# First hop of a graph propagation kernel: two-block groups at both ends, and one-hots that keep their place in program order

## The chip, the cores and the metric

The kernel runs on one core of one Trainium2 chip. A core has a matrix engine (PE, with its weight loads shown apart as PEld), a vector engine (DVE), an activation engine (ACT), a general engine (POOL) and a queue engine (SP) that starts transfers. The metric is the device time of one execution in microseconds, as the median of several runs. A profile of one execution gives the times of single instructions.

## The reference

Seven hops of a normalised sum over the edges of a graph, then a small attention over the eight vectors that each node has, and a readout. N is 10,000 nodes, E 160,000 edges, D 128. The hops are all that matters here.

```
h = x
toks = [x]
for _ in range(K):                                   # K = 7
    msg = h[src] * deg_inv_sqrt[src, None] * deg_inv_sqrt[dst, None]
    h = _segment_sum(msg, dst, N)
    toks.append(h)
tok = jnp.stack(toks, axis=1)                        # (N, K+1, D)
t = _layernorm(tok, axis=-1)
...
return jnp.einsum('nk,nkd->nd', alpha, o)
```

## The kernel before

The edges are sorted first, by source and by destination block, into cells (pass A and a decode, 0 to 394 us). A hop then works on blocks of 128 destination nodes: 78 blocks (NW) and a last remainder block. For a block, matmuls with selection matrices gather the source rows out of the table in on-chip memory (L667, into `p`), copies bring them to 16 bits (`eb`, L670, on ACT or DVE), and matmuls with a second set of selection matrices add them into the sum of the block (`acc`, L645). Edges for which a cell has no room are fetched row by row from DRAM (`og`, L591, on POOL) by an index `oidx`, and added by L631 and L658 (with the matrix `Sov`). `finish` (L617) adds the two halves of the sum on DVE, and L696 to L698 write the table's new rows and the row maximum `mx`.

The first hop builds these selection matrices (`w`, both sets in one tile) while it runs, and stores them to DRAM (`gsd`), from where hops 2 to 7 load them. It works in groups of blocks, called quads in the code: 20 groups, of blocks 72–75, 76–77, then 0–3, 4–7 up to 68–71. Iteration q of the loop runs four generators, a step of each in turn: `place` for group q+1, `left_out` for group q, `matrices` for group q, and the hop itself (`hop1`) for group q−1.

`place` takes the blocks of a group in pairs. For a pair, on each engine:

- DVE: the one-hot `oh` of the cell of each edge (128 x 3800 numbers; L396, made in `onehot`, L204), in a pool with two buffers
- PE: the counts of each cell, 25 matmuls (L400); ACT copies them to H (L401); PE makes their running sums (L406); ACT copies them to U (L408)
- DVE: `ux`, the one-hot times U (L217); PE sums over the cells (L222, L223); DVE reduces to the rank `rk` of each edge in its cell (L226)
- DVE: the one-hot of the rank and two products with it (`R`, L204 and L210), then the edges without room (`vo`, L423; L425)
- PE: the matrix of cells times ranks, 50 matmuls (L420) from `oh` and `R`; ACT copies it to `tbs` (L421)

At the end of a group the table goes to DRAM (`srow`, L430), and PE spreads it (L434, L436); DVE writes `oidx` (L439). `left_out` starts with the flags `fl` (L448), once a group, and gives the index and the matrix for the edges without room (L451 to L481, with `ohp` at L204 and matmuls at L473). `matrices` reads the rows back (`rb`, L555) and writes `w`: the gather half by L582 on DVE or two activations on ACT (L578), the scatter half by L571 and L583 on DVE. `w` has five buffers. `place_end` (up to L544) does the like for the edges of the remainder block at the end, with twelve one-hots `ohp` and matmuls L537.

Each engine runs its instructions in one fixed order. A scheduler of the language sets it, from its own estimate of when each instruction's inputs are ready; an instruction may be moved ahead of others that the program states first. `keep_in_program_order(x)` ties an instruction behind the one that the program stated just before it on the same engine.

Of the kernel before, what the change touches and what calls it, by code (L numbers as in the profile page):

```python
# [15 lines left out]
ALU = mybir.AluOpType  # L16
# [6 lines left out]
NG = 18  # L23
# [9 lines left out]
NS = 4 * NJ  # L33
# [3 lines left out]
NW = NT - 1  # L37
NE = 3
# [5 lines left out]
class Hops:  # L44
# [152 lines left out]
        V.tensor_scalar(self.ctok[0], self.disT, self.sinv, None, op0=ALU.mult)  # L197


    def onehot(self, pool, name, key, n, oh=None):  # L200
        m = key.shape[1]
        if oh is None:
            oh = pool.tile([128, m, n, 2], F16, name=name)
        self.nc.vector.tensor_tensor(oh, key[:, :, None, :].to_broadcast([128, m, n, 2]),  # L204
                                     self.io2[:, None, :n, :].to_broadcast([128, m, n, 2]), op=ALU.is_equal)
        return oh

    def times(self, out, oh, f):
# [160 lines left out]

    def pb_open(self, c):  # L370
        tc, V = self.tc, self.nc.vector
        self.bwp = c.enter_context(tc.tile_pool(name="bw", bufs=2))
        self.bw1 = c.enter_context(tc.tile_pool(name="bw1", bufs=1))
        self.pU = c.enter_context(tc.tile_pool(name="pU", bufs=1, space=PSUM))
        tm = c.enter_context(tc.tile_pool(name="psm", bufs=1, space=PSUM)).tile([128, 2, 128], F32, name="tm")
        self.tb, self.msc = tm[:NS, 0, :].rearrange("p (g r) -> p g r", g=2), tm[:, 1, :]

        cp = self.bp
        es = cp.tile([NS, 4, NJ], I32, name="es")
        self.nc.gpsimd.iota(es, pattern=[[1, 4], [4, NJ]], base=0, channel_multiplier=-1)  # L380
        self.io4 = cp.tile([128, 32, 2], F16, name="io4")
        V.tensor_copy(self.io4, self.iof[:, :32, None].to_broadcast([128, 32, 2]))
        self.pidn = cp.tile([128, 1], F32, name="pidn")
        V.tensor_scalar(self.pidn, self.pid1, -STEEP, 1.0, op0=ALU.mult, op1=ALU.add)
        self.esel = cp.tile([NS, 4, NJ], F16, name="esel")
        V.tensor_scalar(self.esel, es, 0.0, None, op0=ALU.is_equal)

    def place(self, ts, got):

        tc, nc, V, A, T, G = self.tc, self.nc, self.nc.vector, self.nc.scalar, self.nc.tensor, self.nc.gpsimd  # L390
        wp, w1, n = self.bwp, self.bw1, len(ts)
        tbs = wp.tile([NS, 4, 64], F16, name="tbs")
        ov = wp.tile([128, 4, 8], F32, name="ov")
        for p0 in range(0, n, 2):
            cols = lambda z: z[:, :, ts[0] + p0:ts[0] + p0 + 2]
            oh = self.onehot(wp, "oh", cols(self.kB), NS)  # L396
            ur = self.pU.tile([128, 512], F32, name="ur")
            H = wp.tile([128, NS, 2], F16, name="H")
            for c in range(NCH):
                T.matmul(ur[:, :2 * NS], self.id16, oh[:, c], start=c == 0, stop=c == NCH - 1)  # L400
            A.copy(H, ur[:, :2 * NS].rearrange("p (k i) -> p k i", i=2))  # L401
            yield
            U = ur[:, 512 - 2 * NS:].rearrange("p (k i) -> p k i", i=2)
            h = NS // 4
            for w in range(4):
                T.matmul(U[:, w * h:(w + 1) * h], self.triw[:, w, :], H[:, w * h:(w + 1) * h], start=True, stop=True)  # L406
            U2 = wp.tile([128, NS, 2], F16, name="U2")
            A.copy(U2, U)  # L408
            yield
            yield from self.rank(wp, w1, ur, oh, U2, cols(self.wB))  # L410
            rk = self.rk
            R = w1.tile([128, NCH, 2 * CAP, 2], F16, name="R")
            ro = self.onehot(w1, "R", rk, CAP, R[:, :, :CAP])
            self.times(R[:, :, CAP:], ro, cols(self.dl))
            self.times(ro, ro, cols(self.sl))
            yield
            tb = self.tb
            for g in range(2):
                for c in range(NCH):
                    T.matmul(tb[:, g, :], oh[:, c, :, g], R[:, c, :, g], start=c == 0, stop=c == NCH - 1)  # L420
            A.copy(tbs[:, p0:p0 + 2, :], tb)  # L421
            vo = wp.tile([128, NCH, 2], F32, name="vo")
            V.scalar_tensor_tensor(vo, rk, float(CAP), cols(self.TT), op0=ALU.is_ge, op1=ALU.mult)  # L423
            for g in range(2):
                V.max(ov[:, p0 + g, :], vo[:, :, g])  # L425
            yield
        n, a, b = len(ts), ts[0], ts[-1] + 1
        msc = self.msc

        nc.sync.dma_start(self.srow[a:b, :].rearrange("t (s r) -> s t r", r=CAP), tbs[:4 * NG, :n, 0:CAP])  # L430
        dsl = wp.tile([128, 4, NJ], I32, name="dsl")
        for g in range(n):
            for q in range(4):
                T.matmul(msc[32 * q:32 * q + 32, 32 + g * NJ:32 + (g + 1) * NJ], tbs[:, g, CAP:2 * CAP], self.esel[:, q, :],  # L434
                         start=True, stop=True, tile_position=(0, 32 * q))
                T.matmul(msc[32 * q:32 * q + 32, 16 + g * NI:16 + (g + 1) * NI], tbs[:, g, 0:CAP], self.esel[:, q, NG:],  # L436
                         start=True, stop=True, tile_position=(0, 32 * q))
        A.activation(dsl[:, :n, :], msc[:, 32:32 + n * NJ].rearrange("p (g j) -> p g j", j=NJ), AF.Copy, bias=-1.0)
        V.tensor_scalar(self.oidx[:, a:b, :NI], msc[:, 16:16 + n * NI].rearrange("p (g i) -> p g i", i=NI), -1.0, 0.0, op0=ALU.add, op1=ALU.max)  # L439
        got += [dsl, ov]  # L440
# [266 lines left out]
    def run(self, ctx, beside, nhop=K):  # L707
        tc, nc, V, A, T, G = self.tc, self.nc, self.nc.vector, self.nc.scalar, self.nc.tensor, self.nc.gpsimd
        with ExitStack() as c:
# [2 lines left out]
            G.memset(self.TT[:, :, NK:], 0.0)  # L712
            self.pass_a()
            self.decode()
            self.gsp = c.enter_context(tc.tile_pool(name="gs1", bufs=5))
            self.pg = c.enter_context(tc.tile_pool(name="pg1", bufs=4, space=PSUM))
            self.pacc = c.enter_context(tc.tile_pool(name="pc1", bufs=2, space=PSUM))
            self.ogp = c.enter_context(tc.tile_pool(name="og1", bufs=2))
            self.fp = c.enter_context(tc.tile_pool(name="fp1", bufs=1))
            self.pb_open(c)  # L720
            self.more_ebufs(c.enter_context(tc.tile_pool(name="eb1", bufs=1)), 5, True)
            pend = []
# [4 lines left out]
                self.next_rows(t, s, self.tab[1], self.c1[1], self.mx[0], 1, nc.sync)  # L727
                self.token_out(1, t, s, self.ctok[0])

            quads = [list(range(a, min(NW, a + 4))) for a in (4 * NG, 4 * NG + 4, *range(0, 4 * NG, 4))]  # L730
            dsl, W, nq = [[] for _ in quads], [[] for _ in quads], len(quads)

            def hop1(q):
                for t, w in zip(quads[q], W[q]):
                    og = [self.fetch(t, j, (self.tabd[0], self.tabh[0])) for j in range(NI + 1)]
                    yield from self.block(t, w, self.tab[0], lambda og=og: og, pend, 4, (4, 5), True,
                                          lambda jj: q < nq - 1 or jj in (0, 2, 4, 5, 7), fin1, t == quads[0][0])
                    if t == quads[-1][1]:
                        pend.append(lambda: self.end_block(True, fin1))

            for _ in self.place(quads[0], dsl[0]):
# [1 line left out]
            for q in range(nq + 1):  # L743
                pl = self.place(quads[q + 1], dsl[q + 1]) if q + 1 < nq else self.place_end() if q + 1 == nq else iter(())
                lf = self.left_out(quads[q], dsl[q][1]) if q < nq else iter(())
                if q + 1 == nq:
                    pl, lf = chain(lf, pl), iter(())
                if q == nq:
                    for k in range(NE):
                        self.fetch_end(k, self.tabd[0])  # L750
                if q == 0:
                    mt = self.matrices(quads[0], dsl[0][0], W[0])
                    next(mt)
                hp = hop1(q - 1) if q else iter(())
                for i in range(16):
                    if i % 2 == 0:
                        next(hp, None)
                    if i % 3 != 1:
                        next(pl, None)
                    if i % 2 == 1:  # L760
                        next(lf, None)
                    if i in (1, 3, 7, 9, 11, 15):
                        next(mt, None)
                for g in (pl, lf, mt, hp):
                    for _ in g:
                        pass
                if q + 1 < nq:
                    mt = self.matrices(quads[q + 1], dsl[q + 1][0], W[q + 1])
                    next(mt)
# [8 lines left out]
        with ExitStack() as c:  # L778
# [24 lines left out]
            for k in range(2, nhop + 1):  # L803
                i = k % 2
# [622 lines left out]
```

## Time and profile before

| | us |
|---|---|
| median of 3 runs | 4046.76 |
| lowest and highest run | 4042.29, 4049.51 |
| the profiled execution | 4058.61 |
| its span on the core | 4056.8 |
| pass A and decode | 0 to 394 |
| first hop | 394 to 1132 |
| hops 2 to 7 | 1132 to 3530 |
| attention and readout | 3530 to 4057 |

Over the whole span PE is busy 91%, PEld 74%, DVE 75%, ACT 69%, POOL 45%, and the mean granted clock of PE was 0.976 of the full one. A timeline row reads: start, duration, engine, line, operation, output and inputs with their shapes, how many instructions the row holds, and in brackets the idle time of the engine ahead of it with what ended it. A row of waits reads: engine, output and line that waited, what it waited for, total us, how often, the longest. The flags row (L448) comes once a group and so marks the groups in time.

### The profile page before, as it was taken

To read this page: it belongs to the slowest core of one execution; us is meant where nothing else is said; L and a number is where in the kernel's file an instruction comes from. 1 tells how busy PE (TensorE), PEld (TensorE's weight loads), DVE (VectorE), ACT (ScalarE), POOL (GpSimd) and SP (SyncE) were. 2 spreads that over 40 slices of the span, in tenths; PEclk is the share of its full clock that TensorE was granted. 3 is DMA by queue.
4 is the path that set the end of the run, shared out by engine and by line. 5 is a ranking of instruction groups with operands and counts; after the bars stand their busy time and mean duration, and the time that the engine had idled before them with its cause. 6 is when DMAs were issued, how large, how long until landed. Compare 5 with 4: busy or idle time off the path is not lost.

```text
span 4056.8 us, 165985 instructions
## 1 busy us (share of the span) xinstructions
PE 3686.9 (91%) x69041; PEld 3015.9 (74%) x69041; DVE 3041.1 (75%) x6960; ACT 2781.9 (69%) x6927; POOL 1837.6 (45%) x2493
## 2 busy tenths in 40 slices
PE   4776899999889999999999999999999999999996
PEld 3765677777667777777777777777777887888885
DVE  8999888888766666666666666666664555999998
ACT  6674577777656666666666666666666668888884
POOL 0000244444455556555655565565556662222222
PEclk8888999999999999999999999999999999999997
DMA  3100455555466666666666666666667661222220
GB/s 99 35 1 1 154 169 169 173 164 173 144 183 181 186 185 184 184 185 183 186 184 186 183 184 183 184 186 184 185 181 222 186 184 53 72 77 79 73 73 24
DMA packets 320875, 590.64 MB, mean 146 GB/s; under 512 B 56767, under 2 KB 214685, under 8 KB 314861
## 3 DMA queue, kind: packets, MB, share of 16 engines
q1 hardware_dynamic: 281213, 501.46, 39.4%
q0 software_dynamic: 35616, 73.01, 8.3%
q8 instruction: 542, 8.88, 0.9%
q10 hardware_dynamic: 3280, 5.45, 0.5%
q14 instruction: 224, 1.84, 0.1%
HBM read 451.66 MB, written 128.06 MB: 143 GB/s over the span
## 4 chain that ended last, share of the span: by engine, by line
PE 62%; DVE 25%; issue 4%; another core or an unknown queue 4%; DMA 3%; ACT 2%; POOL 0%; DVEq 0%; SPq 0%; POOLq 0%; ACTq 0%
PE p L667 20%; PE acc L645 19%; DVE eb L670 5%; PE acc L631 3%; PE pv L1087 3%; PE po L1098 2%; PE pu L1076 2%; PE ta L341 2%; DVE s L617 2%; PE tm L420 2%; DVE R L210 2%; DVE oh L204 1%; PE pt L1066 1%; DVE tab L696 1%
## 5 line engine op out<-in xcount | busy, mean ns | idle before, releaser
L670 ACT CAST eb<-p 128x512 f16<-128x512 f32 x3494 | 1819.8, 601 | 851.9 <-PE p L667 515.0
L667 PE MATMUL p<-tab,w 128*32 128x256 f16 x39312 | 1309.8, 275 | 117.9 <-DVE eb L670 69.0
L667 PEld LDWEIGHTS <-w 128*32 128x32 fp8e3 x39312 | 996.8, 96 | 350.4 <-issue 295.0
L645 PE MATMUL acc<-eb,w 128*128 128x256 f16 (+1 forms) x9828 | 1199.3, 273 | 1.0 <-issue 0.6
L645 PEld LDWEIGHTS <-w 128*128 128x128 fp8e4 x9828 | 948.7, 98 | 152.5 <-issue 38.2
L670 DVE CAST eb<-p 128x512 f16<-128x512 f32 x1420 | 929.4, 686 | 112.8 <-PE p L667 97.1
L591 POOL DMA_INDIRECT og<-tabh,oidx x546 | 602.7, 1104 | 374.5 <-POOL og L601 181.1
L617 DVE TENSOR_REDUCE s<-acc 128x128 f32<-128x256 f32 x553 | 234.1, 423 | 676.3 <-PE acc L645 385.3
L591 POOL DMA_INDIRECT og<-tabd,oidx x546 | 552.7, 1012 | 307.2 <-issue 138.4
L703 POOL TENSOR_SCALAR r<-s,ctok 128x128 f32<-128x128 f32 x553 | 391.9, 709 | 561.3 <-DVE s L617 492.0
L327 ACT ACTIVATE o<-oh,d2s 128x79 f16<-128x79 f16 x800 | 204.8, 373 | 81.2 <-PE ta L341 81.2
L1112 ACT ACTIVATE junk<-tab 128x128 f32<-128x128 f32 x625 | 245.1, 394 | 0.0
L1098 PEld LDWEIGHTS po<-v,pT 128*128 128x128 f32 x1250 | 160.0, 194 | 43.9 <-issue 27.6
L341 PE MATMUL ta<-o,ro 128*128 128x158 f16 x1250 | 120.9, 269 | 77.9 <-DVE ro L337 77.9
L1170 POOL TENSOR_TENSOR p<-e,in 128x512 f32<-128x512 f32 (+1 forms) x40 | 40.8, 1019 | 331.8 <-DVE e L1168 300.2
L697 DVE SCALAR_TENSOR_TENSOR tab<-s,c,tab 128x128 f16<-128x128 f32 x474 | 170.2, 359 | 14.6
L1087 PE MATMUL pv<-Wv,xT 128*128 128x131 f32 x1250 | 176.0, 284 | 5.0 <-ACT xT L1067 4.1
L341 PEld LDWEIGHTS <-ro 128*128 128x128 f16 x1250 | 115.8, 114 | 82.2 <-DVE ro L337 82.1
L1098 PE MATMUL po<-v,pT 128*128 128x128 f32 x1250 | 167.9, 278 | 6.8 <-DVE o L1104 6.8
L1087 PEld LDWEIGHTS pv<-Wv,xT 128*128 128x128 f32 x1250 | 153.2, 191 | 21.9 <-issue 8.2
L125 POOL MEMSET eb<- 128x520 f16 x10 | 8.2, 851 | 341.1 <-PE ta L341 341.1
L631 PE MATMUL acc<-og,w 128*128 128x256 f16 x546 | 153.9, 282 | 0.0
(314 smaller groups left out, 4641.9 us busy)
## 6 DMA issues: line engine op xcount, KB each, us to landing
w<-gsd SPq DMA_DIRECT2D x468, 592.0 KB
gsd<-w SPq DMA_DIRECT2D x78, 592.0 KB
rb<-srow SPq DMA_DIRECT2D x78, 576.0 KB
tok<-r SPq DMA_DIRECT2D x546, 64.0 KB
tab<-tok SPq DMA_DIRECT2D x273, 128.0 KB
tabd<-tab SPq DMA_DIRECT2D x469, 64.0 KB
og<-tabh,oidx POOLq DMA_INDIRECT x546
og<-tabd,oidx POOLq DMA_INDIRECT x546
```

Source lines behind the costliest of these rows:

```text
L327: A.activation(o[:, j - a, NK:, i], oh[:, j, :, i], AF.Copy, scale=d2s[:, c0:c0 + 1])
L341: T.matmul(ta, ro[:, j - a, :, i], o[:, j - a, :, i], start=j + i == 0, stop=j + i == NP)
L591: self.nc.gpsimd.indirect_dma_start(out=o, out_offset=None, in_=src[0] if i == NI else src[1], in_offset=bass.IndirectOffsetOnAxis(ap=self ...
L617: self.nc.vector.tensor_reduce(s, acc[:, 0:256].rearrange("p (h d) -> p d h", h=2), axis=X, op=ALU.add)
L631: T.matmul(acc[0][:, :256], W, og()[i], start=start, stop=stop)
L645: T.matmul(acc[0][:, :m], w[:, J * 128:(J + 1) * 128], e[:, j, :m], start=first and J == 0, stop=J == NG - 1 and not (first or late))
L667: T.matmul(p[32 * q:32 * q + 32, j], w[:, NJ * 128 + s * CAP:NJ * 128 + (s + 1) * CAP].bitcast(F8G), tab[:, s, :], start=True, stop=True)
L670: (A.copy if evac(jj) else V.tensor_copy)(e[:, :n, 0:256], p[:, :n].rearrange("p j h d -> p j (h d)"))
L703: self.nc.gpsimd.tensor_scalar(r, s, ct[:, t:t + 1], None, op0=ALU.mult)
L1087: T.matmul(p[:, g - a, :], S[i]["xT"][:, g, :], Wv, start=True, stop=True)
L1098: T.matmul(p[:, g - a, :], PT[i % 2][:, g, :], S[i]["v"][:, g, :128], start=True, stop=True)
L1112: A.activation(j, S[i]["x"][:, g, :], AF.Square, bias=S[i]["x"][:, g, 0:1], scale=-1.0, accum_out=S[i]["sq"][:, g:g + 1])
```

## The change

Three things. First, `onehot` takes `pin`, and `place` sets it for `oh`: the instruction keeps its place in the program behind the DVE instruction that was stated just before it. In the first pairs that is `oidx` (L439), an `ohp` or `Sov`; from the sixth pair on it is the row maximum `mx` (L698) of a hop block. Second, the groups: a group of two blocks stands first and two of two blocks last. There are 21: 72–73, 74–77, 0–3 up to 64–67, 68–69, 70–71. What the last group had (DVE taking a share of the copies `eb`) now belongs to the last two groups, with four blocks as before; the remainder block's sum is appended after block 70, and its fetches are issued after the first step of the last hop group. Third, five pools are made with `reuse_waits="tile"`: an instruction that reuses memory of an earlier pool waits for the tile that it takes, not for the pool.

```
-    def onehot(self, pool, name, key, n, oh=None):
+    def onehot(self, pool, name, key, n, oh=None, pin=False):
...
+        if pin:
+            self.tc.keep_in_program_order(made)
...
-        self.bwp = c.enter_context(tc.tile_pool(name="bw", bufs=2))
-        self.bw1 = c.enter_context(tc.tile_pool(name="bw1", bufs=1))
+        self.bwp = c.enter_context(tc.tile_pool(name="bw", bufs=2, reuse_waits="tile"))
+        self.bw1 = c.enter_context(tc.tile_pool(name="bw1", bufs=1, reuse_waits="tile"))
...
-            oh = self.onehot(wp, "oh", cols(self.kB), NS)
+            oh = self.onehot(wp, "oh", cols(self.kB), NS, pin=True)
...
-            quads = [list(range(a, min(NW, a + 4))) for a in (4 * NG, 4 * NG + 4, *range(0, 4 * NG, 4))]
+            ends = [4 * NG, 4 * NG + 2, NW], [*range(0, 4 * NG - 3, 4), 4 * NG - 2, 4 * NG]
+            quads = [list(range(a, b)) for e in ends for a, b in zip(e, e[1:])]
...
-                                          lambda jj: q < nq - 1 or jj in (0, 2, 4, 5, 7), fin1, t == quads[0][0])
-                    if t == quads[-1][1]:
+                                          lambda jj: q < nq - 2 or jj in (0, 2, 4, 5, 7), fin1, t == quads[0][0])
+                    if t == quads[-1][0]:
                         pend.append(lambda: self.end_block(True, fin1))
...
-                if q == nq:
-                    for k in range(NE):
-                        self.fetch_end(k, self.tabd[0])
...
                     if i % 2 == 0:
                         next(hp, None)
+                    if q == nq and i == 0:
+                        for k in range(NE):
+                            self.fetch_end(k, self.tabd[0])
```

The pools gs1, og1 and fp1 get the same argument. The lines of the changed kernel stand two lower than before from L206 on, so L217 is L219 there, and L698 is L700.

On DVE, a group of four blocks in the middle, around the second pair of the group that is being placed. Before:

```order
L210 TENSOR_TENSOR R<-R,dl 128x25x64
L425 MAX ov<-vo 128x8 x2
L210 TENSOR_TENSOR R<-R,sl 128x25x64
L204 TENSOR_TENSOR ohp<-ph,io_217 128x1024
L204 TENSOR_TENSOR oh<-kB,io_217 128x3800
L617 TENSOR_REDUCE s<-acc 128x128
L582 TENSOR_SCALAR w<-rb,pid_219 128x2304
```

Now:

```order
L584 TENSOR_SCALAR w<-rb,pid_219 128x2304
L619 TENSOR_REDUCE s<-acc 128x128
L204 TENSOR_TENSOR ohp<-ph,io_217 128x1024
L698 TENSOR_SCALAR tab_64<-s,c_246 128x128
L585 TENSOR_TENSOR w<-hit,byte 128x608
L699 SCALAR_TENSOR_TENSOR tab_64<-s,c_246,tab_64 128x128
L700 TENSOR_REDUCE mx_241<-tab_64 128x1
L204 TENSOR_TENSOR oh<-kB,io_217 128x3800
L204 TENSOR_TENSOR ohp<-ph,io_217 128x1024
```

The one-hot stood right behind the first pair's `R` (and one `ohp`); it now stands behind `R`, a third matrix of the group and a whole hop block's close. In the order before, this one-hot belongs to the pair after the next; in the order now, to the next `ux`.

Still on DVE, in the same group, from the second pair's `ux` to its rank. Before:

```order
L217 TENSOR_TENSOR ux<-oh,U_12977 128x3800
L204 TENSOR_TENSOR ohp<-ph,io_217 128x1024
L583 TENSOR_TENSOR w<-hit,byte 128x608 x2
L617 TENSOR_REDUCE s<-acc 128x128
L696 TENSOR_SCALAR tab_64<-s,c_246 128x128
L697 SCALAR_TENSOR_TENSOR tab_64<-s,c_246,tab_64 128x128
L698 TENSOR_REDUCE mx_241<-tab_64 128x1
L226 TENSOR_REDUCE rk<-ur 128x50
```

Now:

```order
L700 TENSOR_REDUCE mx_241<-tab_64 128x1
L204 TENSOR_TENSOR ohp<-ph,io_217 128x1024
L219 TENSOR_TENSOR ux<-oh,U_12977 128x3800
L228 TENSOR_REDUCE rk<-ur 128x50
L204 TENSOR_TENSOR R<-rk,io_217 128x25x64
L425 SCALAR_TENSOR_TENSOR vo<-rk,TT 128x50
```

Seven instructions lay between `ux` and `rk`; now none does, and rows of the same kinds stand between `oh` and `ux`.

On ACT, a middle group, around the second pair's counts H. Before:

```order
L421 CAST tbs<-tm 76x128
L670 CAST eb_5251<-p 128x2x256
L670 CAST eb_5253<-p 128x2x256
L726 COPY indeg<-acc 128x1
L401 CAST H<-ur 128x152
L408 CAST U_15605<-ur 128x152
```

Now:

```order
L580 ACTIVATE w<-rb,pidn 128x1152
L728 COPY indeg<-acc 128x1
L580 ACTIVATE w<-rb,pidn 128x1152
L403 CAST H<-ur 128x152
L672 CAST eb_257<-p 128x2x256
L410 CAST U_14729<-ur 128x152
```

H now stands behind both halves of a matrix (L578 before, L580 now), and one copy stands between H and U.

More of the change, by code (lines that the diff above doesn't have):

```diff
@@ L203, in onehot @@
             oh = pool.tile([128, m, n, 2], F16, name=name)
-        self.nc.vector.tensor_tensor(oh, key[:, :, None, :].to_broadcast([128, m, n, 2]),
-                                     self.io2[:, None, :n, :].to_broadcast([128, m, n, 2]), op=ALU.is_equal)
+        made = self.nc.vector.tensor_tensor(oh, key[:, :, None, :].to_broadcast([128, m, n, 2]),
+                                            self.io2[:, None, :n, :].to_broadcast([128, m, n, 2]), op=ALU.is_equal)
+        if pin:
+            self.tc.keep_in_program_order(made)
         return oh
@@ L714, in run @@
             self.decode()
-            self.gsp = c.enter_context(tc.tile_pool(name="gs1", bufs=5))
+            self.gsp = c.enter_context(tc.tile_pool(name="gs1", bufs=5, reuse_waits="tile"))
             self.pg = c.enter_context(tc.tile_pool(name="pg1", bufs=4, space=PSUM))
             self.pacc = c.enter_context(tc.tile_pool(name="pc1", bufs=2, space=PSUM))
-            self.ogp = c.enter_context(tc.tile_pool(name="og1", bufs=2))
-            self.fp = c.enter_context(tc.tile_pool(name="fp1", bufs=1))
+            self.ogp = c.enter_context(tc.tile_pool(name="og1", bufs=2, reuse_waits="tile"))
+            self.fp = c.enter_context(tc.tile_pool(name="fp1", bufs=1, reuse_waits="tile"))
             self.pb_open(c)
```

## The prediction

> **What bounds the kernel now.** I read the windows first, because the change touches one stage of several, then the waits of that stage, then the timeline of one of its groups. The first hop runs from about 394 to 1132 us. Its even middle, from the flags of group 4 (a DVE row of L448, written once a group) to those of group 18, is 14 groups of four blocks.
>
> ```profile
> core 0: us, PE busy (x) PEld busy (x) DVE busy (x) ACT busy (x) POOL busy (x), PEclk, DMA share, GB/s
> 531.22:1024.31 493.09, 458.39 (x8826) 372.06 (x8824) 433.08 (x826) 365.53 (x796) 231.74 (x168) 1.00 0.52 170
> ```
>
> In the middle PE is busy 93%, DVE 88%, ACT 74%. A group takes 493.09/14 = 35.22 us, in which PE works 32.74, DVE 30.93; DVE is idle 4.29. What it waits for in that stretch, and two of the costs of its rows:
>
> ```profile
> DVE oh L204 <- PE tm L420: 40.6, 27, 1.6
> ...
> L204 DVE TENSOR_TENSOR oh<-kB,io 128x3800 f16<-128x3800 f16 x28 | 59.8, 2137 | 40.6 <-PE tm L420 40.6
> L217 DVE TENSOR_TENSOR ux<-oh,U 128x3800 f16<-128x3800 f16 x28 | 59.6, 2129 | 7.6 <-ACT U L408 3.7 <-ACT eb L670 2.4 <-issue 1.6
> ```
>
> So 40.6 of 60 us of DVE idleness is one wait: the one-hot `oh` of a coming pair stands on DVE ahead of everything else, and cannot be written until L420 has read the buffer of the pair two before (two buffers). That is 40.6/14 = 2.90 us a group. The change goes at this wait, by putting `oh` later. Here is what surrounds it, in the second half of one group:
>
> ```profile
> 752.59 2.14 DVE L217 TENSOR_TENSOR ux<-oh,U 128x3800 f16<-128x3800 f16 x1 [0.53 <-ACT eb L670]
> 754.78 1.86 PE L222 MATMUL ur<-ux,id 128*128 128x250 f16 x16 [0.83 <-DVE ux L217]
> 756.46 0.23 PE L223 MATMUL ur<-wB,id 128*128 128x50 f16 x1
> 756.73 0.42 DVE L226 TENSOR_REDUCE rk<-ur 128x50 f16<-128x250 f32 x1
> 759.63 0.97 DVE L210 TENSOR_TENSOR R<-R,sl 128x1600 f16<-128x1600 f16 x1
> 760.65 2.00 PE L420 MATMUL tm<-R,oh 128*76 128x64 f16 x50 [0.38 <-DVE R L210]
> 762.69 2.14 DVE L204 TENSOR_TENSOR oh<-kB,io 128x3800 f16<-128x3800 f16 x1 [1.49 <-PE tm L420]
> 763.02 1.06 PE L645 MATMUL acc<-eb,w 128*128 128x257 f16 x8
> 764.06 1.81 PE L400 MATMUL ur<-oh,id 128*128 128x152 f16 x25
> 765.70 0.34 PE L473 MATMUL tm<-dg,ohp 128*128 128x3 f16 x8
> 765.90 0.28 ACT L401 CAST H<-ur 128x152 f16<-128x152 f32 x1 [0.55 <-PE ur L400]
> 766.61 0.29 ACT L408 CAST U<-ur 128x152 f16<-128x152 f32 x1 [0.42 <-PE ur L406]
> 767.81 2.12 DVE L217 TENSOR_TENSOR ux<-oh,U 128x3800 f16<-128x3800 f16 x1
> 771.81 2.43 ACT L578 ACTIVATE w<-rb,pidn 128x1152 fp8e3<-128x1152 f16 x2
> ```
>
> The reader is to see a chain that runs through three engines for every pair: `oh` (2.1 us) on DVE, counts L400 on PE, H on ACT, L406 on PE, U on ACT, `ux` on DVE, rank sums L222 and L223 on PE, `rk` on DVE. From the start of L400 to the end of U it took 766.90 − 764.06 = 2.84 us, from the end of `ux` to the earliest `rk` 756.73 − 754.73 = 2.00 us. While this runs, DVE needs other work.
>
> **The change, middle groups.** Each has two pairs. *Removed:* both waits of `oh`, 2.90 us a group, since now L420 of the pair in hand has long read the buffer when `oh` comes up: at its new place `oh` stands behind a whole L420 and the close of a hop block. *Added:* nothing in count; but DVE's rows stand otherwise, and the wait moves to what is late next. I walked the new DVE order with the durations above and below:
>
> - first pair, `oidx` of L480: its input comes from L473, which PE now has behind four of the counts of L400, these behind `oh`. Four counts (4 × 1.81/25, with the delay of the last about 0.4), L473 0.34 and the copy L476 on ACT 0.3 are 1.1 us after `oh`; five small DVE rows of about 0.1 cover 0.45: **0.67**.
> - first pair, `ux`: 2.6 us of DVE rows stand between it and `oh` against the 2.84 of counts to U, less what ran ahead: **0.07**.
> - the third matrix of a group, L582: its buffer (one of five) is read by the scatter L645 that PE runs behind L420. From the end of R at 760.60 to L645's end at 764.03 are 3.4 us; DVE has w L583 and hit L571 (0.7 each) as cover; if only part of the eight matmuls reads that buffer, 1.0 to 2.0: I take **1.56**.
> - second pair, `ux`: H stands on ACT behind both halves of a w activation of L578 (2.43 the two), U and `ux` behind it: **0.45**.
> - second pair, `rk`: it stands directly behind `ux`; before, seven rows lay between. Nothing covers the 2.00 (and up to 0.1 of PE's gathers in hand): **2.1**.
>
> That is 4.85 us a group. Before, DVE's idleness was 4.29, and 4.85 + 30.93 = 35.78 us a group: **+0.56 each, +8 for 14**. PE's 32.74 leave it room.
>
> The bounds of this term. Best: all new waits are covered by reordering between engines that I count as exposed, and DVE comes down to what the kernel already shows between its own flags at 497.70 and 531.22, 33.5 us: 14 × (33.5 − 35.22) = −24. Worst: the wait for `rk` holds the tail of the pair (R, L420, the closes behind it) and w L583 and hit keep their old waits as well (0.5 a group), with H late by a whole activation (1.0 more): 36.7 to 37.2, so +21 to +28.
>
> ```profile
> 465.14 0.17 DVE L448 TENSOR_SCALAR fl<-ov 128x32 f16<-128x32 f32 x1
> 497.70 0.17 DVE L448 TENSOR_SCALAR fl<-ov 128x32 f16<-128x32 f32 x1
> 531.22 0.18 DVE L448 TENSOR_SCALAR fl<-ov 128x32 f16<-128x32 f32 x1
> 1024.31 0.17 DVE L448 TENSOR_SCALAR fl<-ov 128x32 f16<-128x32 f32 x1
> ```
>
> [...]
>
> **The start.** A two-block group comes first, so its flags come a pair earlier (about 404 instead of 413.73), and the first hop block can close sooner: before, Sov and the first fetch waited for `oidx` of L480.
>
> ```profile
> 394.36 2.13 DVE L204 TENSOR_TENSOR oh<-kB,io 128x3800 f16<-128x3800 f16 x1
> 396.99 2.14 DVE L217 TENSOR_TENSOR ux<-oh,U 128x3800 f16<-128x3800 f16 x1 [0.39 <-PE W L260]
> 402.58 0.42 DVE L226 TENSOR_REDUCE rk<-ur 128x50 f16<-128x250 f32 x1 [3.46 <-PE ur L223]
> 413.73 0.17 DVE L448 TENSOR_SCALAR fl<-ov 128x32 f16<-128x32 f32 x1
> 426.35 0.17 DVE L448 TENSOR_SCALAR fl<-ov 128x16 f16<-128x16 f32 x1
> 437.34 0.16 DVE L480 SCALAR_TENSOR_TENSOR oidx<-lo 128x4 int32<-128x4 f32 x1
> 438.54 6.02 DMA og<-tabd,oidx
> 445.02 0.42 DVE L617 TENSOR_REDUCE s<-acc 128x128 f32<-128x256 f32 x1 [4.18 <-PE acc L658]
> ```
>
> I walked the new DVE order from 402.58 on: R to 406; the tied second `oh` has to wait for `oidx` L439 of the first group (L420 2.0, copy, L436; 2.4 us of idle DVE); then two one-hots, two `ux` and a rank, 16.5 us, until L480 at about 425.8, 11.5 earlier. The price: the second pair starts 12 us later than before (`oh` ran at 394.36), so flags 1 come at about 432 instead of 426. Flags 2 come at about 457 instead of 465, with two block closes fewer done (1.3 us of DVE each: s, two tab, mx), flags 4 at about 528 instead of 531: **−3** (−7 to +1). A pool's reuse waits, now by tile, can only touch the 0.39 of `ux` above.
>
> **The end.** After the last L420 there remain the closes of six blocks, not nine, as the last full group has become two of two; the extra group adds 13 DVE rows of 0.1 to 0.7 us and one more round trip of srow.
>
> ```profile
> 1059.72 2.00 PE L420 MATMUL tm<-R,oh 128*76 128x64 f16 x50 [0.17 <-DVE R L210]
> 1078.14 1.42 DVE L582 TENSOR_SCALAR w<-rb,pid 128x2304 fp8e3<-128x2304 f16 x1 [4.08 <-DMA rb<-srow]
> 1080.55 0.35 PE L473 MATMUL tm<-dg,ohp 128*128 128x3 f16 x8 [2.21 <-DVE ohp L204]
> 1111.09 0.61 PE L667 MATMUL p<-tab,w 128*32 128x256 f16 x8 [2.27 <-ACT eb L670]
> 1124.31 0.27 PE L133 MATMUL pm<-ident,c 128*1 128x128 f32 x1 [2.38 <-DVE c L882]
> ```
>
> From the flags of group 18 to L133 were 100.0 us. Removed: the wait of 4.08 for rb and the 2.21 that hang on it, if the matrices of the last two blocks come while six others are still open. Given back: the tail's ohp to L537 trips, of which now six stand bare (about 0.4 to 0.6 each beyond their work), and the second wait for rb (srow's write and read, within the other's 4.08). **−2** (−6 to +4).
>
> Nothing after 1132 changes. **Sum:** +8 − 3 − 2 = +3. The profiled execution took 4058.61 us, 12 above the median of the runs, 4046.76; the difference is taken to the median: **4050 us**. A difference under 0.2% (8 us) can't be told from none here.
>
> **The rivals.**
>
> *DVE gets its waits back.* The slack of the other engines absorbs the new order, and DVE, freed of 2.90 a group, reaches the 33.5 of the group at 497.70. For it: that group has the rows of the others, and in it `oh` waited for L420 only once, for 0.40; PE's 32.74 allow it. Against: there `oh`, s and the tabs stood between `ux` and `rk` and covered the rank, and the bare 2.0 of the new order takes most of 2.90.
>
> ```profile
> 499.54 2.14 DVE L204 TENSOR_TENSOR oh<-kB,io 128x3800 f16<-128x3800 f16 x1 [0.40 <-PE tm L420]
> ```
>
> Its price is −24 −3 −2 = −29, or 4018; half of that, if one of the two pairs regains its wait, 4032; typically 4025. Chance 0.27.
>
> *Each pair's chain lies bare* (the other side). With `oh` one pair ahead instead of two, counts, H, U, `ux` and `rk` of the second pair must run inside the last third of the group. The place is `ux` with `rk` directly behind it and H behind L578. The price: the 4.85 above, and H late by one half of the w activations more than I walked (2.43/2, so 1.2 at most, 1.0 taken). That is 36.8 a group, 14 × (36.8 − 35.22) = +22, and with the ends +17: 4064. It decides from a group of 36.2 on, where 14 × 0.98 less 5 passes the 8 us that can be told. For it: `rk` waited 3.46 for PE at 402.58, where nothing covered it, and in the row at 765.90 H already waited for PE with no activation ahead of it. Against: PE has 2.5 us of slack a group to run the counts at once, and the added 1.0 is a cost that I did not find in the walk. Chance 0.35.
>
> *The tie does nothing.* If `oh` keeps its old place, the middle stays at 35.22 and only the ends move: 4042 to 4046. The order of the changed program shows `oh` behind mx (L698) in every middle group, so this has 0.04, counted with the forecast.
>
> *The clock* is no rival but a check on the start: PE stood still before 444.61, and the rows behind it ran slow (32 gathers in 1.90 us; at 756.62, at full clock, 40 took 1.55).
>
> ```profile
> 444.61 0.37 PE L658 MATMUL acc<-og,Sov 128*128 128x256 f16 x1 [4.45 <-DMA og<-tabd,oidx]
> 445.12 1.90 PE L667 MATMUL p<-tab,w 128*32 128x256 f16 x32
> ...
> 756.62 1.55 PE L667 MATMUL p<-tab,w 128*32 128x256 f16 x40
> ```
>
> An earlier first fetch can only shorten this stand; some 3 us of slow rows stand behind it, which is the size of the start's bounds. In the middle no new wait of PE is over 1 us, and the granted clock there was 1.00.
>
> **How the numbers follow.** Forecast 4050, with its own range 4040 to 4057, 0.38 (the 0.04 of a tie that does nothing among it); faster rival 0.27; slower rival 0.35. The range leaves out the outer ends of both rivals, about a tenth on each side: 4024 to 4068. Faster than 4039: 0.27 and the lowest of the forecast, 0.28. Slower than 4055: 0.35 and the top of the forecast, 0.38. Between them 0.34.
>
> **What would show it.** In the changed kernel: no wait of `oh` for L420; `rk` L226 waiting about 2 us for L223 once a group; L582 waiting for PE; the spacing of the L448 rows, 35.8 by the sum, 33.5 by the first rival, over 36 by the second; Sov's first fetch near 426; L420 to L133 at the end shortened by one group of closes. The prediction is wrong if `rk` waits under 0.5 us, or if a wait turns up on PE or ACT (gathers L667 for eb) that is larger than those on DVE.

## The result, and the profile after

The changed kernel takes 4097.14 us (4094.12 to 4099.4) against 4048.14 us before (4042.29 to 4050.58): a ratio of 1.0122, with a 95% interval of 1.0109 to 1.0135. It is about 49 us slower. The forecast was 4050; the rival with the bare chain, which ends on the same side, gave 4064.

The flags (L448, now L450) divide the loss. At the flags of group 4 the changed kernel stands at 536.54 instead of 531.22 (+5.3). From there to the flags of group 18, 14 groups with the same work, it needs 530.57 instead of 493.09 (+37.5). From there to L133 it needs 1171.62 − 1067.11 = 104.5 instead of 100.0 (+4.5). That is 47.3 us. Behind L133 the profiled execution of before took 11.0 us longer than that of the changed kernel (2932.5 against 2921.5), so the two profiled executions lie only 36.3 us apart; that of before was 10.5 above the median of its kernel. The middle, as a window (the same columns as in the prediction), and what DVE and PE wait for in it (us in total, times, the longest):

```profile
536.54:1067.11 530.57, 470.95 (x8895) 375.27 (x8893) 437.01 (x827) 365.91 (x801) 199.54 (x168) 0.99 0.46 157
```

```profile
DVE rk L228 <- PE ur L225: 32.1, 21, 2.0
DVE oidx L441 <- ACT dsl L440: 15.2, 13, 1.2
DVE w L584 <- PE acc L658: 12.1, 9, 1.5
DVE w L584 <- DMA rb<-srow: 10.6, 4, 3.0
DVE ux L219 <- ACT U L410: 8.0, 15, 0.9
```

```profile
PE acc L660 <- DMA og<-tabd,oidx: 16.8, 13, 2.5
PE tm L475 <- DVE oidx L441: 13.2, 13, 1.0
PE ur L402 <- DVE oh L204: 9.8, 14, 1.0
```

A group is 37.90 us. DVE works 31.21 of them (30.93 before) and is idle 6.68 (4.29 before). The waits of `oh` are gone. In their place stands a list in which only `rk` is over 2: 2.3 for `rk`, 1.1 for `oidx`, 0.9 and 0.8 for the matrices of L584, 0.6 for `ux`. PE, which had no wait for a fetch in the middle before, has one of 1.2 us a group. One group's second pair, from the timelines of DVE, PE and ACT:

```profile
862.89 0.28 DVE L700 TENSOR_REDUCE mx<-tab 128x1 f32<-128x128 f16 x1
863.09 2.12 DVE L204 TENSOR_TENSOR oh<-kB,io 128x3800 f16<-128x3800 f16 x1
865.26 1.81 PE L402 MATMUL ur<-oh,id 128*128 128x152 f16 x25 [0.57 <-DVE oh L204]
868.12 0.31 ACT L403 CAST H<-ur 128x152 f16<-128x152 f32 x1
869.13 2.14 DVE L219 TENSOR_TENSOR ux<-oh,U 128x3800 f16<-128x3800 f16 x1 [0.91 <-ACT U L410]
873.28 0.42 DVE L228 TENSOR_REDUCE rk<-ur 128x50 f16<-128x250 f32 x1 [2.00 <-PE ur L225]
876.87 1.99 PE L422 MATMUL tm<-R,oh 128*76 128x64 f16 x50 [0.29 <-DVE R L212]
```

The one-hot stands right behind a row maximum, as the tie says, and from there the pair's chain runs to L422, 13.8 us later. DVE has two `ohp`, a `w` and the fourth block's close beside it, and still stands 0.91 for U and 2.00 for the rank. What comes behind L422 can be read in the chain of waits (start, us, what):

```profile
839.18 2.00 PE tm L422 x50
...
843.79 0.17 DVE oidx L441
843.97 0.04 issue
844.01 0.35 PE tm L475 x8
...
844.59 0.17 DVE oidx L482
844.76 0.26 issue
845.02 5.12 DMA og<-tabd,oidx
850.14 0.04 issue
850.18 0.27 PE acc L660
```

The index of this fetch hangs on the L422 of the pair in hand, and PE then stands in front of L660. Before, PE had no wait for `og` in the middle.

### The profile page after: what moved, and what is told of

It is laid out like the page before. It is cut to its first block, busy times and chain, and to the rows that moved or that the text cites. A ratio compares the mean times of both kernels' runs of the same rounds, so it can differ in the third digit from the quotient of the medians.

```text
span 4093.1 us, 165931 instructions
## 1 busy us (share of the span) xinstructions
PE 3699.1 (90%) x69042; PEld 3018.6 (74%) x69042; DVE 3045.1 (74%) x6973; ACT 2785.3 (68%) x6934; POOL 1804.1 (44%) x2493
## 4 chain that ended last, share of the span: by engine, by line
PE 58%; DVE 24%; DMA 5%; issue 4%; another core or an unknown queue 4%; ACT 4%; POOL 0%; SPq 0%; DVEq 0%; ACTq 0%; POOLq 0%
PE p L669 19%; PE acc L647 18%; DVE eb L672 6%; PE acc L633 3%; PE pv L1090 2%; DMA og<-tabd,oidx 2%; PE po L1101 2%; PE pu L1079 2%; PE ta L343 2%; DVE s L619 2%; DVE ux L219 2%; PE tm L422 1%; PE ur L224 1%; ACT eb L672 1%
## 5 line engine op out<-in xcount | busy, mean ns | idle before, releaser
L593 POOL DMA_INDIRECT og<-tabh,oidx x546 | 583.6, 1069 | 362.7 <-POOL og L603 173.5
L593 POOL DMA_INDIRECT og<-tabd,oidx x546 | 542.2, 993 | 362.4 <-issue 121.0
```

Source lines behind the costliest of these rows:

```text
L593: self.nc.gpsimd.indirect_dma_start(out=o, out_offset=None, in_=src[0] if i == NI else src[1], in_offset=bass.IndirectOffsetOnAxis(ap=self ...
```

## The experiments

Ratios are to the kernel before on the same chip; the chips differed (before took 3882 to 4065 us), so whole times are compared by ratio alone. "A group" is the mean from the flags of group 4 to those of group 18 in the profile.

**1. The tie alone, and everything else alone.** The first run adds `pin=True` and `keep_in_program_order` to the kernel before. The second takes it out of the changed kernel:

```
-            oh = self.onehot(wp, "oh", cols(self.kB), NS, pin=True)
+            oh = self.onehot(wp, "oh", cols(self.kB), NS)
```

> The kernel before with the tie alone: old groups of four and two, old pools. Theory T (the tie makes the groups longer, in every group alike): a group of about 37.7 us instead of 35.2, so 15 groups x 2.5 = +38, between +30 and +50 us in all, 0.8 to 1.2% slower than before. Rival G (the new groups and the pools' waits shift the order, and the tie matters little): within 10 us of before.

> The changed kernel without the tie: new groups and pool waits remain. Theory T: groups of 35.2 us again, and only the ends move, -10 to +8 us against before. Rival G: still +30 us or more.

Measured: 1.0101 (1.0085 to 1.0118), a group of 36.96; and 0.9996 (0.9987 to 1.0006), a group of 35.36. The loss is the tie's. On the old groups its middle is shorter than expected (36.96, not 37.7), and its start 13.4 longer (flags of group 4 at 544.65). Without the tie the start is 7.0 us shorter (524.19) and the end 5.3 longer (105.3), which with +2 in the middle cancels.

**2. The tie on one pair of each group.** `pin=p0 == 0` and `pin=p0 == 2`.

> The changed kernel with the tie on the first pair of each group alone. If the loss sits in the first pair (four counts that wait for the one-hot stand on PE ahead of L475, so oidx, the fetch and the matmul L660 behind it come late: about 1.0 + 1.2 us a group, and H 1.0), the middle keeps most of its +2.7 us a group, 36.8 to 37.9, +22 to +38 us. If it sits in the second pair (bare rank, 2.0, and U late, 0.9), the group falls to 35.2 to 36.0, at most +12 us.

> The changed kernel with the tie on the second pair alone. First-pair theory: a group of 35.2 to 36.0 us, at most +12 us against before. Second-pair theory (the 2.0 us for which rk waits behind ux has no other row, and the third matrix waits 1.3): 36.8 to 37.9 us a group, +22 to +38.

Measured: first pair 0.9997 (0.9987 to 1.0008), a group of 35.00; second pair 1.0120 (1.0104 to 1.0137), 37.74. The whole loss belongs to the second pair. The first run also answers what the wait of `oh` had cost; its window and DVE's largest waits:

```profile
529.40:1019.41 490.01, 464.78 (x8862) 371.43 (x8863) 430.73 (x827) 363.15 (x799) 282.77 (x168) 1.00 0.52 170
```

```profile
DVE oidx L441 <- ACT dsl L440: 37.4, 14, 2.7
DVE w L585 <- PE acc L658: 12.4, 14, 0.9
DVE oidx L482 <- ACT lo L478: 3.2, 14, 0.2
```

There is no wait of `oh` left, but DVE is idle (490.01 − 430.73)/14 = 4.23 us a group, as before; `oidx` now waits 2.7 a group. Of the 2.90 us only 0.36 came, against the run without a tie.

**3. Single waits taken away.** First the fetch: its indices come from block 72, long ready.

```
-                    og = [self.fetch(t, j, ...) for j in range(NI + 1)]
+                    og = [self.fetch(4 * NG if j == NI and q > 2 else t, j, ...) for j in range(NI + 1)]
```

> The changed kernel, but from the fourth group on the second row fetch of every block in the first hop takes its indices from block 72, which are there long before (so the sums of the first hop are not the reference's); the fetch itself stays. Ring theory: the tie closes a ring (row maximum of a block, one-hot, counts, H, U, ux, rank, R, L422, oidx, L482, fetch of the next block, L660, row maximum), and its time is the group's; the fetch, some 4 us of it, now falls out: a group of 35.2 to 36.5 us, +5 to +28 us against before. Row theory (what counts is the bare rank of 2.0 us and the other waits of DVE; PE's 1.2 us for the fetch costs little): 37.4 to 37.9 us a group, +40 to +52.

Then the bare rank, with `keep_in_program_order` on the reduction into `rk`:

> The changed kernel with the rank rk tied as well, behind the DVE row that the program states just before it: seven rows of other work then stand between ux and rk and cover the 2.0 us. Row theory: 2.0 us a group less, 35.7 to 36.4, +12 to +25 us against before. Ring theory: rk comes no sooner than before, so 36.8 to 38.0 us a group, +30 to +50.

Measured: 1.0084 (1.0067 to 1.0101), a group of 37.54; and 1.0108 (1.0091 to 1.0125), 37.33. PE no longer waited for the fetch in the one, and `rk` had rows ahead of it in the other, yet only 0.4 and 0.6 us came off (the first run's total, +34 us, lies between its two ranges). The first run speaks against the ring through the fetch, the second against the bare rank as the price. Both edits at once, and then with the token's store on POOL's queue as well, with that edit alone as a control:

```
-        self.nc.sync.dma_start(self.tok[k][...], r[:n])
+        (self.nc.gpsimd if k == 1 else self.nc.sync).dma_start(self.tok[k][...], r[:n])
```

> The rank tied behind other rows and the early index of block 72, both at once (the sums of the first hop are not the reference's). Each alone took 0.4 to 0.6 us off a group of 37.9. If two rings of nearly the same length were there (one through the fetch, where PE waits 1.5 us and DVE's s behind it 1.8; one through the bare rank), both gone give 35.2 to 36.2 us a group, +2 to +20 us against before. If the gains only add, as they do when the pair's chain as a whole is what DVE walks through, 36.8 to 37.2, +28 to +38.

> As the run before (rank tied behind other rows, early index of block 72), and the store of a block's token (tok<-r) started from POOL's queue and not from SP's: there the reads rb<-srow of the next group stood 3.4 us behind a store that waited for POOL, and the first matrix and ux waited 1.6 and PE 2.4 us behind them. If several rings of nearly one length hold the late pair, this was the next: 35.3 to 36.6 us a group, +2 to +25 us against before. If the late pair's chain as a whole is the cost, whatever single wait is taken away: 37 or more, +30 or more.

> The kernel before with the token's store on POOL's queue alone, as the control of that edit: by both theories within 10 us of before, since there L582 waits for rb only 1.7 us in 14 groups; slower if POOL's fetches are held up by the stores.

Measured: 1.0125 (1.0108 to 1.0142), a group of 37.66; 1.0092 (1.0074 to 1.0110), 37.21; and the control 1.0005 (0.9995 to 1.0015). With both edits the gains did not even add (37.66 lies outside both ranges), and with the third the group stayed over 37. The control shows that the third edit is not free: its middle is 35.61 a group, 0.39 more than before, and its start 7.6 shorter. Differences under 1 us between these runs are blurred by PE's clock: the run with the early index has a stretch at half clock in seven groups (mean 38.2; the other seven 36.9), the changed kernel in two of 14 (39.2 and 37.7). In the groups at full clock alone, the early index, the tied rank, both, and all three leave 36.9, 37.1, 37.5 and 37.0. Taking waits away one after another did not bring the time back. The chain of waits of the run with all three shows what took their place:

```profile
832.08 2.01 PE tm L423 x50
834.11 0.27 ACT tbs L424
834.40 0.32 SPq L433
...
836.76 5.55 DMA rb<-srow
842.31 0.02 issue
842.33 0.69 DVE w L585
843.02 0.65 issue
843.67 2.14 DVE ux L219
```

Behind the same L422 (here L423) hangs a second way: the table's rows go to DRAM and come back (`srow`, `rb`) for the group's first matrix, which DVE has ahead of the first pair's `ux`.

**4. The place of the one-hot.** The next pair's one-hot stated and tied behind `ux` of the pair in hand; the second pair's one-hot stated beside the first pair's L422; the second pair's steps two steps later.

```
+        self.oh_next = None if self.ahead is None else self.onehot(wp, "oh", self.kB[:, :, self.ahead:self.ahead + 2], NS, pin=True)
```

> The changed kernel with the one-hot of the next pair (over the group's end too) stated and tied right behind ux of the pair in hand, so that it is a pair ahead again, covers the rank, and waits for no L422. If DVE's waits set the pace before the change, as I predicted from: 33.0 to 33.8 us a group, -20 to -35 us against before. If PE sets it and DVE's waits only move: 34.6 to 35.3 us a group, -12 to +4.

> The changed kernel with both ties kept, but the second pair's one-hot stated five steps earlier, beside the first pair's L422: it then stands ahead of the first pair's ux and not behind the third block's row maximum. If the cost is the place (the second pair's chain can only start after the third block has closed, 14 us ahead of the flags): 34.7 to 35.5 us a group, -8 to +6 us against before. If a tie as such costs (the scheduler has less freedom, other waits): 36.5 or more, +20 or more.

> The changed kernel with the second pair's steps two steps later in the program. By the order the tie then binds the one-hot to a w of L585 ahead of the third matrix, half a block sooner on DVE than in the changed kernel, while its counts, ux and rank come later; seven rows cover the rank. If the place of the one-hot decides: 35.3 to 36.5 us a group, +2 to +22 us against before. If what decides is how late ux and rank stand in the group: 37 or more, +30 or more.

Measured: 1.0023 (1.0012 to 1.0033), a group of 35.91; 1.0009 (1.0000 to 1.0018), 35.33; 1.0131 (1.0115 to 1.0146), 37.83. A tie as such costs nothing (second run). The third run told the one-hot from the rest of the chain: the one-hot stood sooner, but `ux` later, and the loss was whole. The first run was slower than either theory said: DVE was idle 5.11 a group.

**5. Only `ux` late.** No one-hot is tied; they run a pair ahead as before. The second pair's `ux` is stated one or two steps later and tied.

```
+            for _ in range(1 if p0 else 0):
+                yield
             yield from self.rank(wp, w1, ur, oh, U2, cols(self.wB))
...
+        if self.late:
+            self.tc.keep_in_program_order(made)
```

> The changed kernel with no one-hot tied, but the second pair's ux stated one step later and tied: it stands behind the fourth block's row maximum, with rk directly behind, while its one-hot, counts, H and U are ready long before, a pair ahead. If the place of the one-hot is what costs (its counts, H and U inside the last third): 35.2 to 36.3 us a group, within 15 us of before. If the place of ux (the end of the pair's chain after the fourth close) is: 37 to 38.5, +30 to +55.

> As the run before, with two steps: ux stands behind the fourth block's first table row and three rows cover the rank; again the one-hot is free and a pair ahead. Place of the one-hot: 35.2 to 36.3 us a group. Place of ux: 36.8 to 38, +25 to +50.

Measured: 1.0185 (1.0167 to 1.0202), a group of 39.73; and 1.0177 (1.0157 to 1.0198), 39.01. This is more than the change itself costs, with early one-hots, and more than the ranges given for a late `ux`. Part of it is the clock: in all 14 groups of both runs it fell to half for a time, 78.5 and 68.3 us in all. Had PE lost half of that time whole, 2.8 and 2.4 us a group, 36.9 and 36.6 would be left (an estimate from these numbers), still over the 35.36 without a tie. The waits of the first of them, over 465 us, 11.7 groups:

```profile
DVE rk L230 <- PE ur L227: 63.0, 23, 3.8
PE acc L668 <- DMA og<-tabd,oidx: 47.0, 11, 5.9
...
DVE oh L204 <- PE tm L430: 7.5, 12, 0.6
```

PE waits 4.0 us a group for the fetch, three times as long as in the changed kernel.

**6. The parts that lost nothing.** A short group at the start alone, without ties; and the same with the tie on the first pair.

```
+            ends = [4 * NG, 4 * NG + 2, NW], [*range(0, 4 * NG + 1, 4)]
```

> The changed kernel without ties, and with a short group at the start alone: the last group has four blocks as before. From the other runs: the start is 7 us shorter (flags of group 4 at 524 instead of 531), the middle 35.2 to 35.4 a group, the end 100 instead of 104 to 105: -7 us against before, between -10 and 0. If the short end is not what costs at the end: -2 to +3.

> The parts that lost nothing, put together: the tie on the first pair alone, a short group at the start alone, the last group of four as before. From the runs: start -2, middle 14 x (35.0 - 35.22) = -3, end 0: -5 us against before, between -9 and +2; that would be at the edge of what can be told. If the parts don't add: 0 to +5.

Measured: 0.9998 (0.9989 to 1.0007) and 1.0005 (0.9997 to 1.0014). No version beats the kernel before by what can be told. In the first the start is 6.7 us shorter as expected, and the middle, at 35.47 a group, gives 3.5 of them back. In both the end takes 98.7 to 98.9 us, against 103.7 to 105.3 in the runs that end in two groups of two and lose nothing in the middle: the short end costs some 5 to 6.5 us. Its three parts (two short groups, the later issue of the remainder's fetches, the share of the copies) were not run apart.

## Why the prediction was wrong

**What was right.** The order that the tie makes, and its largest wait in place and size: `rk` directly behind the second pair's `ux` waits 2.0 (2.1 forecast). `ux` for a late U waits 0.6 (0.52 forecast for both pairs), the matrices for a sum of PE 1.1 (1.56 forecast). The wait of `oh` for L420 is gone. The rival "each pair's chain lies bare" had the place (the second pair's `ux` with `rk` behind it) and the sign; its price was +17, and +49 came. That its 36.8 a group is nearer is in part luck: the 1.0 that it added for a late H is not in the trace, where all of `ux`'s waits are 0.6.

**The step that failed** is the sum of the middle, "4.85 + 30.93 = 35.78 us a group": DVE's idleness came to 6.68, not 4.85, and its work to 31.21. The five waits of the walk were not too small. As measured they are 2.30 (`rk`), 0.57 (`ux`), 1.12 (L584 for a sum of PE) and 0.19 (`oidx` of L482, 0.67 forecast), 4.2 in all. The other 2.5 us a group, 35 us in 14 groups, are waits that the walk put at nothing: `oidx` of L441 for `dsl` 1.09, the matrices for `rb` 0.76, `po` 0.38, and small gaps. The sum also let the five waits stand for all of DVE's idleness of 4.29, though the change was to remove only 2.90 of it, and gave no reason for the other 1.39. To carry these 1.39 along would have given 37.17 a group. That is nearer, but not for the right reason: two of those waits, 0.5 us a group, are gone in the changed kernel. Before they were:

```profile
DVE w L583 <- PE acc L656: 4.1, 14, 1.0
DVE hit L571 <- ACT word L566: 2.9, 9, 0.3
```

**The walk stopped at the group's end.** What it left out is what a late pair does to the next group: L441 waits 1.1 for `dsl`, the matrices 0.8 for `rb`, and PE waits 1.2 for the fetch. The walk had only 0.67 at L480 (now L482) there, and said that "no new wait of PE is over 1 us"; L660's reached 2.5.

**The cover counted as gain was none.** "both waits of `oh`, 2.90 us a group" was no price. With them gone and nothing else lost (the tie on the first pair) DVE was idle 4.23 instead of 4.29, and the group 35.00; with both ties at the earlier place it was idle 4.33. In both runs `oidx` waits 2.67 a group in their place: the wait only changed its row. The Trainium skill ("Perfetto Trace Analysis", Identifying the Most-Contended Engine) says to optimize the engine with the highest occupancy first, and to judge the headroom of TensorE by measures such as the busy share of its weight loads. In the middle before, that engine is DVE (88%, against 372.06/493.09 = 75% for the weight loads), but with its wait for `oh` gone and `ux` not late the group was 0.03 to 0.50 us shorter than in the like run without a tie (both ties earlier; the tie on the first pair with the old end), or 0.55 longer (the first run of experiment 4). The rule does not tell what such a wait is worth.

**What the loss is.** Shown: it is the second pair's tie, and it follows how late the second pair's `ux` stands on DVE. Where `ux` stands behind the third block's row maximum with, almost always, at most one row between (25.4 to 26.1 us behind the flags, by the mean of the 14 groups), groups take 34.97 to 35.91. Where the late one-hot and two `ohp` stand between (29.1 to 29.7), they take 36.96 to 37.66; behind rows of the fourth block (29.6 to 31.8), 37.54 to 39.73. A tie as such costs nothing, and the one-hot need not be late for the loss. Shown too is that none of the three waits that were taken away carries it: with fetch, rank and store eased a group still took 37.21. What I argue, and no run isolates, is why the rest stays. The loop from L422 over `srow` and `rb`, or over `oidx` and the fetch, to the next first pair, and on through DVE to the next L422, would then have several ways of nearly the same length. How its 37 us divide among them stays open.

**Start and end.** Both had the wrong sign in the changed kernel: +5.3 instead of −3, +4.5 instead of −2. Without the tie the start is −7.0, so the −3 failed through the tie: groups 3 and 4 took 40.16 and 35.33 us, where before they took 32.56 and 33.52. The end is about the same with the tie or without it (104.5 and 105.3). In the changed kernel the last two groups' flags come 17.89 and 34.24 us apart, 52.1 for what was one group of 35.27, so 16.9 more; the closes saved behind the last flags are worth 12.4 (1171.62 − 1119.25 = 52.4 against 64.7). The forecast saw the second and priced the first far too low. It also had no term for the remainder's fetches: PE stands 4.5 us for them (L614, twice) in the changed kernel and 4.6 to 4.7 in the runs without the tie, with it on the first pair and with it earlier. Before, and with the short start alone, it does not. In the last run, with the old end, it stands 2.8 and the end is as short as before, so how much of the 4.5 is theirs stays open.

## What to carry to other kernels

A wait that one engine shows a group is not yet a price: in this loop its removal only moved it. When two engines hand work to each other, test the removal before counting it. When an instruction is tied to a later place, follow everything that depends on it to the point where the next round starts (a fetch, a round trip through DRAM), and walk that loop, not the tied engine alone. And in a sum of waits, say of each old one whether it stays, and why.

## What the runs showed of the hardware

PE's clock fell after stands shorter than I had expected to matter. In the run with the second pair tied PE stood 3.08 us in front of L660, and in the run with the rank tied 2.49:

```profile
579.84 0.37 PE L660 MATMUL acc<-og,Sov 128*128 128x256 f16 x1 [3.08 <-DMA og<-tabd,oidx]
580.47 2.93 PE L224 MATMUL ur<-ux,id 128*128 128x250 f16 x16
```

```profile
621.25 0.27 PE L661 MATMUL acc<-og,Sov 128*128 128x256 f16 x1 [2.49 <-DMA og<-tabd,oidx]
622.22 3.22 PE L224 MATMUL ur<-ux,id 128*128 128x250 f16 x16
```

The 16 matmuls of L224 took 1.86 us at full clock. The granted clock was 0.50 from 580 to 582 in the one and 0.60 and 0.55 from 622 to 626 in the other. By the Trainium skill ("TensorE: Matmul & The Clock Gate", Part 1) the clock is at half after an idle window of about 3.4 us; here stands of 2.5 were enough, and the measurement decides.

The run with the early index shows that not even that is needed. In its middle PE never stood over 1.07 us, and yet the clock fell to half seven times, for 3.4 us each. One of them:

```profile
689.59 0.34 PE L475 MATMUL tm<-dg,ohp 128*128 128x3 f16 x8 [1.05 <-DVE oidx L441]
689.79 2.47 PE L402 MATMUL ur<-oh,id 128*128 128x152 f16 x21
```

The granted clock was 0.50 from 690.3 to 693.5; the same 21 matmuls took 1.54 us in a group of the changed kernel at full clock. Other stands of 1.0 passed without a fall, so the length of one stand does not decide alone, and no run shows what does.

Over the middle the clock was 0.97 with the second pair tied and 1.00 with the first. The six groups of the former at full clock took 36.4 to 37.1, the eight others 37.6 to 39.8, so part of that run's loss is probably the clock, though a longer stand lengthens a group too. It is not the cause of the loss: in the changed kernel the groups from 577 to 1029 kept the full clock and still took 37.0 to 38.6 us.
